# Conversion of the first weights, place of the fp32 pieces, and h before y in a chain of clustered attention and two wide layers

## The chip, the cores and the metric

The kernel runs on one core of a Trainium2 chip. The metric is the device time of one execution in microseconds (us). Before the change the median of three runs is 830.09 us (829.56 to 830.41). The engines are TensorE (PE in the profile; its weight loads are PEld), VectorE (DVE), ScalarE (ACT), GpSimd (POOL), and SyncE (SP), which here only issues DMAs.

## The reference, cut to what matters

```python
# attention: q, k, v of shape (2, 8, 768, 64), 16 centroids for each head
q_assign = argmax(q_n @ c_n.T); k_assign = argmax(k_n @ c_n.T)
scores = where(q_assign == k_assign, q @ k.T / sqrt(64), -1e9)
attn = exp(scores - max) / (sum + 1e-9)
x = (attn @ v) laid out as (1536, 512)
# layer 1: w_in (512, 2048), w_out (2048, 512)
h = x @ w_in;  x = maximum(0.01 * h, h) @ w_out
# layer 2, of the same shapes, with its own weights
h = x @ w_in;  g = P(h) / (Q(h) + 1e-6);  out = g @ w_out
# P = a0 + a1 h + a2 h^2 + a3 h^3,  Q = 1 + |b0||h| + |b1| h^2
```

The weights arrive as 64-bit floats and are converted in the kernel. Each matrix product is made three times, with high and low parts of both operands, to keep fp32 accuracy.

## The kernel before, in words

**Attention.** Two heads make a pair, and there are 8 pairs. A pair has 12 units of 128 query rows, so there are 96 units (`NU`). `run` (line 662) writes the order of work out by hand, one iteration `i` for each unit. In iteration `i` TensorE transposes the normalised probabilities of unit `i - 4` (`trans_p`, tile `pT`, line 519), computes the scores of unit `i + 1` (`scores`, tile `s`, line 477), and does a third of the products with v of a group of three units (`values`, tile `o`, line 552). VectorE takes the maximum of a row (`nm`, line 486) and the low parts of the probabilities (`pl`, line 538). ScalarE does the exponential (`e`, line 497) and the high parts (`ph`, line 532). GpSimd normalises two units at a time (`normalize`, line 511), after one `denom` on ScalarE and one reciprocal on VectorE for both. In two of three iterations the values stand behind the scores; in the third one they stand in front of them.

The preparation of a later pair is cut into pieces. `plan` (line 404) gives each piece an iteration, counted from the pair's first unit, and a slot in it. Slot `"pe"` comes behind the scores and in front of the values; slot `"act"` comes in front of the exponential; slot `"end"` comes last. `trans` (tile `pa`, line 230, three fp32 transposes) and `sims` (line 307, twelve small fp32 products) stand in slot `"pe"`. All `pT`, `pa`, `sims` and `po` tiles take turns in three PSUM buffers (pool `pq`). `trans_out` on ScalarE (line 233) empties a `pa` tile.

**Weights.** The class `Weights` (line 724) holds a queue of conversions. A piece is a DMA of 512 KB into a tile `st`, then four operations (`conv_a` on ScalarE, line 767; `conv_s` and two `conv_c` on VectorE, lines 774 and 780) that leave fp32 in `wf`, and an end: either a split into high and low parts (ScalarE line 787, GpSimd line 790), or a save of the fp32 weights to DRAM. `step()` does one operation of the queue and loads ahead. Before the change the two inward (`wi`) and two outward (`wo`) pieces of the first group are converted and saved during the attention: their loads are issued in iteration 7, one operation follows in two iterations of three, the last one in iteration 59. After the last preparation piece (iteration 84) the `wi` pieces are read back and split. The saved `wo` pieces are read back too, and split at the start of the layers.

**Layers.** Each layer has its inner dimension in groups of four slices of 128 (the first group is halved). A step has one slice and one block of 384 tokens: `make_h` is 12 matmuls into tile `h` (four PSUM buffers), `back` is the product with `w_out` for the step three earlier (`LAG = 3`), 12 matmuls in layer 1 and 9 wider ones in layer 2, into tiles `y0` to `y3` (one buffer each). In between ScalarE and VectorE (and GpSimd in layer 2) make `gh` and `gl` from `h`; these have three buffers each. `collect` on VectorE adds `y` to `acc` after the last slice of a group. The order of each engine is the order of the calls in the loop at line 1100:

```python
            if i >= LAG:
                back(i - LAG)
            if i < NS:
                make_h(i)
            if 0 <= i - 1 < NS:
                start(i - 1)
```

Of the kernel before, what the change touches and what calls it, by code (L numbers as in the profile page):

```python
# [9 lines left out]
F32 = mybir.dt.float32  # L10
F32R = mybir.dt.float32r
I32 = mybir.dt.int32
AF = mybir.ActivationFunctionType
ALU = mybir.AluOpType
# [3 lines left out]
P = 128  # L18
# [11 lines left out]
def clustered_attention_moe_moe2(  # L30
# [14 lines left out]
    nc = tc.nc  # L45
# [11 lines left out]
    BLK = S // 2  # L57
    QT = BLK // P
# [18 lines left out]
    eps = const.tile([P, 1], F32, name="eps")  # L77
# [46 lines left out]
    UP = HP * T  # L124
    NU = NPAIR * UP
# [6 lines left out]
    class Attention:  # L132
# [62 lines left out]
        def prep_pieces(self, p):  # L195
# [192 lines left out]
            def vsplit(h):  # L388
# [14 lines left out]

            plan = [
                (-27, "end", load_qk),
                (-24, "pe", trans, 0, 0),
                (-23, "act", trans_out, 0, 0),
                (-23, "pe", trans, 0, 1),
                (-22, "act", trans_out, 0, 1),
                (-22, "end", split_hi, 0),  # L410
                (-21, "pe", trans, 1, 0),
                (-21, "end", split_lo, 0, 0),
                (-20, "act", trans_out, 1, 0),
                (-20, "pe", trans, 1, 1),
                (-20, "end", split_lo, 0, 1),
                (-19, "act", trans_out, 1, 1),
                (-18, "pe", sims, 0),
                (-19, "end", split_hi, 1),
                (-17, "act", sims_out, 0),
                (-18, "end", split_lo, 1, 0),  # L420
                (-18, "end", place_a, 0),
                (-17, "end", split_lo, 1, 1),
                (-15, "pe", sims, 1),
                (-14, "act", sims_out, 1),
                (-13, "dve", sims_max),
                (-13, "end", place_a, 1),
# [16 lines left out]
            if p == 1:  # L443
                late = {"sims": (-12, -10), "sims_out": (-11, -9), "sims_max": -9, "is_max": -9,
                        "rank": -9, "first": -8, "onehot": (-7, -6)}
# [12 lines left out]
            if p == 2:  # L458
                late = ("trans", "trans_out", "split_hi", "split_lo")
# [38 lines left out]
                un["e"], un["s"][:, 0:S], AF.Exp, bias=un["nm"], accum_out=un["recip"]  # L498
            )

        def denom(self, u):
            un = self.unit[u]
            nc.scalar.activation(un["sum"], un["sum"], AF.Identity, bias=eps)

        def recip(self, u):
            un = self.unit[u]
            nc.vector.reciprocal(un["sum"], un["sum"])  # L507

        def normalize(self, u):
            un = self.unit[u]  # L510
            nc.gpsimd.tensor_scalar(un["e"], un["e"], un["recip"], 1.0, op0=ALU.mult, op1=ALU.mult)  # L511

        def trans_p(self, u, part):
            un = self.unit[u]
            pp = self.pq.tile([P, 512], F32, tag="pT", name="pT")
            n = T // 2
            for kt in range(n):
                k0 = (part * n + kt) * P
                nc.tensor.transpose(pp[:, kt * P:(kt + 1) * P], un["e"][:, k0:k0 + P], ident)  # L519
            un["pT", part] = pp[:, 0:n * P].rearrange("p (t n) -> p t n", t=n)  # L520
# [24 lines left out]
        def values(self, gi, a, z):  # L545
            p, h, half, _ = self.info(gi * QT)
            gr = self.group[gi]
            if a == 0:
                gr["o"] = self.po.tile([P, BLK], F32, tag="o", name="o")
            for n in range(a, z):  # L550
                kt, j = divmod(n, 2)
                nc.tensor.matmul(  # L552
                    gr["o"],
                    lhsT=self.pair[p]["vs"][:, h * T + tile_of(kt), :],
                    rhs=gr["pl" if j else "ph"][:, kt, :],
                    start=n == 0,
                    stop=n == 2 * T - 1,
                )
# [103 lines left out]
        def run(self, extra, fill):  # L662
            TL = 4
            pieces = {}
            for p in range(NPAIR):
                for i, slot, f in self.prep_pieces(p):
                    pieces.setdefault(max(i, -1), {}).setdefault(slot, []).append(f)
            self.startup(*fill)
            first = -1
            last_prep = max(pieces)  # L670
            n_groups = NU // QT
            part = -(-2 * T // QT)
            for i in range(first, NU + TL + 11):
                def go(slot):
                    for f in pieces.get(i, {}).get(slot, []):
                        f()

                gi, r = divmod(i - TL - 3, QT)
                ok = 0 <= gi < n_groups
                live = 0 <= i - TL < NU  # L680
                go("dve0")
                if 0 <= i < NU:
                    self.row_max(i)
                if i % 2 == 0 and 0 <= i - 2 < NU:
                    self.recip(i - 2)
                    self.normalize(i - 2)
                    self.normalize(i - 1)
                if live:
                    self.trans_p(i - TL, 0)
                    self.hi(i - TL, 0)  # L690
                    self.trans_p(i - TL, 1)
                    self.hi(i - TL, 1)
                if ok and r == QT - 1:
                    self.values(gi, part * r, 2 * T)
                    self.merge_copy(gi)
                go("act")
                if 0 <= i < NU:
                    self.exp(i)
                    if i % 2 == 1:
                        self.denom(i)  # L700
                if 0 <= i + 1 < NU:
                    self.scores(i + 1)
                go("pe")
                if ok and r < QT - 1:
                    self.values(gi, part * r, part * (r + 1))
                if live:
                    self.lo(i - TL, 0)
                    self.lo(i - TL, 1)
                if ok and r == QT - 1:
                    self.merge_add(gi)  # L710
                go("dve")
                gd, rd = divmod(i - TL - 3 - 7, QT)
                if rd == 0 and 0 <= gd < n_groups:
                    self.finish(gd)
                go("end")
                if UP // 2 <= i < NU - 2 * UP and i % 3:
                    fill[1].step()
                if i == last_prep:
                    self.pc.close()
                    extra[0]()  # L720
                elif i > last_prep:
                    extra[1]()

    class Weights:
        def __init__(self, pools):
# [148 lines left out]
            else:  # L874
                weights.add((which, n), weight_source(n, which), which, n % 2, WIDE)

    def queue_scratch(n):
        for which in ("wi", "wo"):
            src = weight_source(n, which)
            t = dram.tile([P, src.shape[1], src.shape[2] // WW], F32, name=f"scratch_{which}{n}")  # L880
            weights.add((which, n), src, which, n % 2, WIDE, store=t)
            scratch[n, which] = t
# [3 lines left out]
    with tc.manual_schedule():  # L886
# [13 lines left out]
        def open_start():  # L900
            def slot(tag):
                def stage():
                    t = xp.tile([P, NCT * BLK], F32, tag=tag, name="xst")
                    return t[:, 0:WR * 1024].bitcast(I32), t[:, WR * 1024:WR * 1536]

                weights.wst.append({"stage": stage, "used": 0, "room": 1})

            if WIDE:
                for j in range(NB // 2, NB):
                    slot(f"xh{j}")  # L910
                    slot(f"xl{j}")
                queue_scratch(0)

        def open_weights(which, par, **kw):
            wpools[which, par] = wctx.enter_context(
# [8 lines left out]
            open_stage("wsta", side="right")  # L924
            queue_group(0)

        def early_step():
            weights.step(1)

        weights = Weights(wpools)  # L930
        with ExitStack() as actx:
# [168 lines left out]
        for i in range(NS + LAG):  # L1100
            if i < NS and steps[i][1:] == (0, 0):
                n1 = steps[i][0] + 1
                begin, total = i, 0
                count = NB * groups[n1 - 1][2]
                if n1 < len(groups):
                    queue_group(n1)
                    if WIDE and n1 + NG - 1 > NG0 and n1 + NG - 1 < len(groups):
                        queue_scratch(n1 + NG - 1)
                    total = weights.pending()
            if i >= LAG:  # L1110
                back(i - LAG)
            if i < NS:
                make_h(i)
            if 0 <= i - 1 < NS:
                start(i - 1)
            if 0 <= i - 2 < NS and rational(i - 2):
                hi(i - 2)
                lo(i - 2)
            if later:
                next_x()  # L1120
            if i >= LAG:
                collect(i - LAG)
            if 0 <= i - 1 < NS and rational(i - 1):
                ratio_end(i - 1)
            due = total * min(i - begin + 1, count - 1) // (count - 1)
            weights.step(max(0, due - (total - weights.pending())))
            if i < LAG and weights.waits_for(("wo", 0)):
                weights.step(4)
            if i == LAG - 2:
                while weights.waits_for(("wo", 0)):  # L1130
                    weights.step()
# [29 lines left out]
```

## Time and profile before

| | us |
|---|---|
| median of three runs | 830.09 |
| the profiled execution, whole | 830.46 |
| its span in the profile | 828.7 |
| PE busy | 797.1 (96%) |
| DVE busy | 649.1 (78%) |
| ACT busy | 533.3 (64%) |
| POOL busy | 398.8 (48%) |

The span has four stages: start-up to about 40 us, attention to about 281 us, layer 1 to about 545 us, layer 2 to the end. Busy times are sums of the durations of instructions. Consecutive matmuls overlap, so the start of a matmul after the start of the one before says more of the pace than its duration. A time in square brackets on a timeline row is the idle time of that engine before the instruction and what ended it.

### The profile page before, as it was taken

Reading aid. Unit: us, or ns where it says so; the run is one execution under the profiler, and the core shown is the slowest. Engines: PE = TensorE matmul, PEld = TensorE weight load, DVE = VectorE, ACT = ScalarE, POOL = GpSimd, SP = SyncE. Lnnn points to the kernel's source line nnn. Section 1 sums busy time; section 2 is a strip of 40 time slices with the busy share of each in tenths; the row PEclk is TensorE's granted clock in tenths of the full one; section 3 lists DMA queues with packets and bytes.
Section 4 is the critical chain, followed back from the end, with each engine's and each line's share of the span. In section 5 each row is a group of like instructions: output and inputs, shape, how many; then the busy total and the mean of one; then the engine's idle time right before and its main releaser. Section 6 shows DMA issues by size and latency. Waiting matters only on the chain.

```text
span 828.7 us, 13356 instructions
## 1 busy us (share of the span) xinstructions
PE 797.1 (96%) x4545; PEld 740.7 (89%) x4545; DVE 649.1 (78%) x1232; ACT 533.3 (64%) x1131; POOL 398.8 (48%) x428
## 2 busy tenths in 40 slices
PE   5898999999999899999999999999999999999997
PEld 4887898898888899999999999997889888988995
DVE  6579989989999557766567556758888878888887
ACT  4588988988989544544253345447666667766664
POOL 5557877877665422331031024256555555554442
PEclk9999999999999999999999999999999999999999
DMA  3775745645410223435544454431111110100112
GB/s 102 175 207 116 169 103 117 170 97 124 106 36 26 102 85 120 131 124 169 165 147 155 141 189 130 150 89 27 35 30 28 38 39 26 26 1 1 40 39 76
DMA packets 42835, 79.80 MB, mean 96 GB/s; under 512 B 5392, under 2 KB 25360, under 8 KB 42768
## 3 DMA queue, kind: packets, MB, share of 16 engines
q1 hardware_dynamic: 42768, 78.96, 33.9%
q8 instruction: 36, 0.59, 0.3%
q14 instruction: 31, 0.25, 0.1%
HBM read 50.37 MB, written 10.49 MB: 73 GB/s over the span
## 4 chain that ended last, share of the span: by engine, by line
PE 50%; POOL 15%; DVE 14%; ACT 10%; issue 8%; DMA 2%; SPq 1%; POOLq 0%; DVEq 0%; ACTq 0%
PE y L961 18%; PE h L961 17%; POOL z L1013 6%; PE o L552 5%; PE pT L519 4%; POOL z L1010 4%; PE s L477 3%; DVE pl L538 3%; DVE nm L486 3%; ACT ln L1026 2%; PE sims L307 2%; ACT r L1027 2%; POOL wol L790 2%; POOL wil L790 2%; DMA st<-in_moe_w_in_dram 1%
## 5 line engine op out<-in xcount | busy, mean ns | idle before, releaser
L961 PE MATMUL h<-xh,wil 128*128 128x384 f32 x512 | 172.2, 336 | 0.0
L961 PE MATMUL h<-xh,wih 128*128 128x384 f32 x512 | 171.9, 336 | 0.0
L961 PE MATMUL h<-xl,wih 128*128 128x384 f32 x512 | 171.8, 336 | 0.0
L995 DVE TENSOR_TENSOR gl<-h,gh 128x384 fp32r<-128x384 f32 x128 | 70.8, 553 | 85.6 <-ACT gh L990 68.0
L511 POOL TENSOR_SCALAR e<-e,sum 128x768 f32<-128x768 f32 x96 | 88.6, 936 | 61.5 <-DVE sum L507 44.4
L790 POOL TENSOR_TENSOR wil<-wf,wih 128x512 fp32r<-128x512 f32 x32 | 41.6, 1308 | 143.8 <-ACT wih L787 143.8
L538 DVE TENSOR_TENSOR pl<-pT,ph 128x384 fp32r<-128x384 f32 x192 | 97.2, 545 | 16.6 <-ACT ph L532 15.5
L961 PEld LDWEIGHTS h<-xl,wih 128*128 128x128 f32 x512 | 96.2, 188 | 2.7
L961 PEld LDWEIGHTS h<-xh,wih 128*128 128x128 f32 x512 | 96.2, 188 | 2.5
L486 DVE TENSOR_REDUCE nm<-s 128x1 f32<-128x768 f32 x96 | 90.9, 947 | 7.3 <-PE s L477 6.8
L961 PEld LDWEIGHTS h<-xh,wil 128*128 128x128 f32 x512 | 96.2, 188 | 0.0
L999 ACT ACTIVATE h<-h 128x384 f32<-128x384 f32 x64 | 30.4, 476 | 98.6 <-PE h L961 98.6
L532 ACT CAST ph<-pT 128x384 fp32r<-128x384 f32 x192 | 82.4, 481 | 17.4 <-PE pT L519 16.2
L497 ACT ACTIVATE e<-s,nm 128x768 f32<-128x768 f32 x96 | 87.3, 909 | 9.4 <-DVE nm L486 5.8
L990 ACT CAST gh<-h 128x384 fp32r<-128x384 f32 x128 | 61.6, 482 | 40.4 <-DVE h L1034 38.3
L961 PE MATMUL y<-gh,woh 128*128 128x384 f32 x256 | 86.1, 336 | 0.1
L961 PE MATMUL y<-gl,woh 128*128 128x384 f32 x256 | 85.8, 335 | 0.2 <-DVE gl L995 0.2
L961 PE MATMUL y<-gh,wol 128*128 128x384 f32 x256 | 85.9, 336 | 0.0
L519 PE MATMUL pT<-ident,e 128*128 128x128 f32 x576 | 81.7, 278 | 2.7 <-DVE pl L538 2.7
L1010 POOL TENSOR_SCALAR z<-y,abv 128x384 f32<-128x384 f32 x64 | 43.2, 676 | 77.6 <-ACT y L1006 70.4
L961 PE MATMUL y<-woh,gh 128*128 128x512 f32 x192 | 76.6, 399 | 2.5 <-ACT gh L990 1.5
L961 PE MATMUL y<-woh,gl 128*128 128x512 f32 x192 | 76.6, 399 | 1.3 <-DVE gl L995 1.0
(104 smaller groups left out, 1855.3 us busy)
## 6 DMA issues: line engine op xcount, KB each, us to landing
st<-in_moe_w_in_dram SPq DMA_DIRECT2D x30, 512.0 KB, 4.6
st<-in_moe_w_out_dram SPq DMA_DIRECT2D x30, 512.0 KB, 4.6
a<-hl SPq DMA_DIRECT2D x56, 192.0 KB, 3.7
b<-hl SPq DMA_DIRECT2D x28, 192.0 KB, 6.0
wf<-scratch_wi SPq DMA_DIRECT2D x14, 256.0 KB, 3.1
wf<-scratch_wo SPq DMA_DIRECT2D x14, 256.0 KB, 3.1
qraw<-in_q_dram SPq DMA_DIRECT2D x16, 192.0 KB, 3.1
kraw<-in_k_dram SPq DMA_DIRECT2D x16, 192.0 KB, 3.2
```

The lines of the kernel that those rows point to most:

```text
L486: nc.vector.reduce_max(un["nm"], un["s"][:, 0:S], axis=AX.X, negate=True)
L497: nc.scalar.activation(un["e"], un["s"][:, 0:S], AF.Exp, bias=un["nm"], accum_out=un["recip"])
L511: nc.gpsimd.tensor_scalar(un["e"], un["e"], un["recip"], 1.0, op0=ALU.mult, op1=ALU.mult)
L519: nc.tensor.transpose(pp[:, kt * P:(kt + 1) * P], un["e"][:, k0:k0 + P], ident)
L532: nc.scalar.copy(un["hi", part], un["pT", part])
L538: nc.vector.tensor_tensor(self.group[gi]["pl"][:, part * n:(part + 1) * n, i * P:(i + 1) * P], un["pT", part], f32(un["hi", part]), op=ALU ...
L790: nc.gpsimd.tensor_tensor(hold["l"][:, i:i + wr, :], hold["wf", i], f32(hold["h"][:, i:i + wr, :]), op=ALU.subtract,)
L961: nc.tensor.matmul(o, lhsT=l, rhs=r, start=(first and idx == 0), stop=(last and idx == n - 1),)
L990: nc.scalar.copy(d["gh"], d["h"])
L995: nc.vector.tensor_tensor(d["gl"], d["h"], f32(d["gh"]), op=ALU.subtract)
L1010: nc.gpsimd.tensor_scalar(d["z"], d["y"], abv[:, 1:2], abv[:, 0:1], op0=ALU.mult, op1=ALU.add)
L1013: nc.gpsimd.tensor_tensor(d["z"], d["z"], d["y"], op=ALU.mult)
```

## The change

The change has five parts.

1. `trans` and `sims` move from slot `"pe"` to a new slot `"pa"`, which is called behind the values (and behind the two `lo` of VectorE). `onehot_t` (tile `po`) stays in `"pe"`.
2. During the attention only the two `wi` pieces of the first group are converted and saved. Their loads are issued in iteration 6; one operation follows in every third iteration from 15 on. The two `wo` pieces are loaded from the input after iteration 84 and converted in place: one `conv_a` falls into iteration 86, the other seven operations into iterations 100 to 106.
3. The last two units have a `denom` and a reciprocal of their own; unit 94 is normalised one iteration earlier on GpSimd, unit 95 on VectorE.
4. The transposed probabilities of unit 95 use the buffers of the scores, and the last group's `o` uses a buffer of `pq` instead of the single one.
5. In the layers `make_h(i)` stands in front of `back(i - 3)`.

```diff
             plan = [
                 (-27, "end", load_qk),
-                (-24, "pe", trans, 0, 0),
+                (-24, "pa", trans, 0, 0),
                 (-23, "act", trans_out, 0, 0),
-                (-23, "pe", trans, 0, 1),
+                (-23, "pa", trans, 0, 1),
...
-                (-20, "pe", trans, 1, 1),
+                (-20, "pa", trans, 1, 1),
...
-        def denom(self, u):
+        def denom(self, u, alone=False):
             un = self.unit[u]
-            nc.scalar.activation(un["sum"], un["sum"], AF.Identity, bias=eps)
+            x = un["recip"] if alone else un["sum"]
+            nc.scalar.activation(x, x, AF.Identity, bias=eps)
...
-            pp = self.pq.tile([P, 512], F32, tag="pT", name="pT")
+            pp = self.ring("pT") if u == NU - 1 else self.ptile("pT")
...
             if a == 0:
-                gr["o"] = self.po.tile([P, BLK], F32, tag="o", name="o")
+                if (gi + 1) * QT == NU:
+                    gr["o"] = self.ptile("o")[:, 0:BLK]
+                else:
+                    gr["o"] = self.po.tile([P, BLK], F32, tag="o", name="o")
...
-                if i % 2 == 0 and 0 <= i - 2 < NU:
+                if NU - 1 <= i <= NU:
+                    self.recip(i - 1, True)
+                    self.normalize(i - 1, (nc.gpsimd, nc.vector)[i - NU + 1])
+                elif i % 2 == 0 and 0 <= i - 2 < NU:
...
                     self.exp(i)
-                    if i % 2 == 1:
+                    if i >= NU - 2:
+                        self.denom(i, True)
+                    elif i % 2 == 1:
                         self.denom(i)
...
                 if live:
                     self.lo(i - TL, 0)
                     self.lo(i - TL, 1)
+                go("pa")
                 if ok and r == QT - 1:
                     self.merge_add(gi)
...
-                if UP // 2 <= i < NU - 2 * UP and i % 3:
+                if i == UP // 2:
+                    fill[1].preload(4)
+                if UP + 3 <= i < NU - 2 * UP and i % 3 == 0:
                     fill[1].step()
...
-                    extra[1]()
+                    extra[1](i >= NU + TL)
...
-                queue_scratch(0)
+                queue_scratch(0, ("wi",))
...
-        def early_step():
-            weights.step(1)
+        def early_step(late):
+            if late or weights.waits_for(("wi", 0)):
+                weights.step(1)
...
+            if i < NS:
+                make_h(i)
             if i >= LAG:
                 back(i - LAG)
-            if i < NS:
-                make_h(i)
```

## Rows read from the trace of the kernel before

**Rows 1.** Busy time by stretch: start:end, length, then PE, PEld, DVE, ACT, POOL, PEclk.
```profile
40.00:236.00 196.00, 187.62 (x1278) 170.39 (x1279) 180.86 (x332) 170.35 (x413) 140.86 (x160) 0.99 0.55 130
236.00:281.00 45.00, 41.22 (x264) 36.78 (x264) 37.11 (x70) 37.65 (x89) 28.99 (x34) 1.00 0.10 29
281.00:545.00 264.00, 263.63 (x1514) 262.97 (x1513) 168.74 (x324) 120.47 (x237) 62.03 (x50) 1.00 0.45 145
545.00:600.00 55.00, 53.10 (x268) 47.22 (x267) 44.95 (x78) 35.67 (x69) 35.40 (x37) 1.00 0.13 38
800.00:828.70 28.70, 23.43 (x111) 19.43 (x109) 21.33 (x39) 13.95 (x26) 8.40 (x10) 1.00 0.15 55
```

**Rows 2.** TensorE's waits, 40 to 236 us: total us, times, longest.
```profile
PE pa L230 <- ACT x L233: 3.5, 11, 0.5
```

**Rows 3.** Timeline of TensorE at one such wait: start, duration, what.
```profile
103.08 0.55 PE L230 MATMUL pa<-ident,kraw 128*128 128x128 f32 x3 [0.51 <-ACT x L233]
103.39 0.42 PE L552 MATMUL o<-ph,vs 128*128 128x384 f32 x1
103.64 0.34 PE L552 MATMUL o<-pl,vs 128*128 128x384 f32 x1
103.82 0.35 PE L552 MATMUL o<-ph,vs 128*128 128x384 f32 x1
```

**Rows 4.** VectorE's longest waits, 40 to 236 us.
```profile
DVE pl L538 <- ACT ph L532: 12.0, 21, 1.8
```

**Rows 5.** Timeline of TensorE: the same piece in four successive pairs.
```profile
80.52 0.47 PE L365 MATMUL po<-identr,oh 128*96 128x128 f32 x4
...
111.28 0.47 PE L365 MATMUL po<-identr,oh 128*96 128x128 f32 x4
...
142.99 0.48 PE L365 MATMUL po<-identr,oh 128*96 128x128 f32 x4
...
174.21 0.47 PE L365 MATMUL po<-identr,oh 128*96 128x128 f32 x4
```

**Rows 6.** Timeline of ScalarE: the first conversion of a weight piece.
```profile
49.20 0.67 ACT L767 ACTIVATE xst<-xst 128x512 f32<-128x512 f32 x1 [1.10 <-DMA xst<-in_moe_w_in_dram]
```

**Rows 7.** Timeline of VectorE and GpSimd: conversions of the outward pieces.
```profile
127.39 0.41 DVE L774 TENSOR_SCALAR xst<-xst 128x512 int32<-128x512 int32 x1
...
128.91 1.81 POOL L511 TENSOR_SCALAR e<-e,sum 128x768 f32<-128x768 f32 x2 [0.24 <-DVE sum L507]
...
130.04 0.95 DVE L774 TENSOR_SCALAR xst<-xst 128x512 int32<-128x512 int32 x1
...
135.77 0.68 DVE L780 SCALAR_TENSOR_TENSOR xst<-xst 128x512 int32<-128x512 int32 x1
```

**Rows 8.** Timeline at the end of attention.
```profile
251.25 3.33 SPq L761 DMA_DIRECT2D wf<-scratch_wo  x2
...
254.34 0.62 PE L477 MATMUL s<-a 128*128 128x512 f32 x2 [0.66 <-ACT e L497]
...
273.77 0.44 PE L552 MATMUL o<-ph,vs 128*128 128x384 f32 x1 [0.40 <-DVE xf L573]
...
278.64 0.45 PE L552 MATMUL o<-ph,vs 128*128 128x384 f32 x1 [1.16 <-DVE xf L573]
```

**Rows 9.** DMA issues, page part 6: count, size, us to landing.
```profile
st<-in_moe_w_in_dram SPq DMA_DIRECT2D x30, 512.0 KB, 4.6
```

**Rows 10.** Timeline in layer 2: its first y, a collect near the end, the last y.
```profile
556.28 0.47 PE L961 MATMUL y<-woh,gh 128*128 128x512 f32 x1 [0.81 <-ACT r L1027]
...
810.89 1.88 DVE L1079 TENSOR_TENSOR acc<-y,acc 128x512 f32<-128x512 f32 x3
...
822.47 0.50 PE L961 MATMUL y<-woh,gh 128*128 128x512 f32 x1 [1.21 <-ACT gh L990]
```

**Rows 11.** Busy time and granted clock in two short stretches; columns as in rows 1.
```profile
44.00:48.00 4.00, 4.00 (x22) 3.79 (x22) 2.20 (x4) 2.26 (x6) 2.25 (x3) 0.57 0.99 253
60.00:62.00 2.00, 2.00 (x15) 1.68 (x14) 2.00 (x6) 1.81 (x5) 1.33 (x2) 1.00 1.10 191
```

More of the change, by code (lines that the diff above doesn't have):

```diff
@@ L405, in prep_pieces @@
                 (-27, "end", load_qk),
-                (-24, "pe", trans, 0, 0),
+                (-24, "pa", trans, 0, 0),
                 (-23, "act", trans_out, 0, 0),
-                (-23, "pe", trans, 0, 1),
+                (-23, "pa", trans, 0, 1),
                 (-22, "act", trans_out, 0, 1),
                 (-22, "end", split_hi, 0),
-                (-21, "pe", trans, 1, 0),
+                (-21, "pa", trans, 1, 0),
                 (-21, "end", split_lo, 0, 0),
                 (-20, "act", trans_out, 1, 0),
-                (-20, "pe", trans, 1, 1),
+                (-20, "pa", trans, 1, 1),
                 (-20, "end", split_lo, 0, 1),
                 (-19, "act", trans_out, 1, 1),
-                (-18, "pe", sims, 0),
+                (-18, "pa", sims, 0),
                 (-19, "end", split_hi, 1),
@@ L422, in prep_pieces @@
                 (-17, "end", split_lo, 1, 1),
-                (-15, "pe", sims, 1),
+                (-15, "pa", sims, 1),
                 (-14, "act", sims_out, 1),
@@ L499, in exp, with recip, normalize @@
             )
-        def denom(self, u):
+        def denom(self, u, alone=False):
             un = self.unit[u]
-            nc.scalar.activation(un["sum"], un["sum"], AF.Identity, bias=eps)
-        def recip(self, u):
+            x = un["recip"] if alone else un["sum"]
+            nc.scalar.activation(x, x, AF.Identity, bias=eps)
+        def recip(self, u, alone=False):
             un = self.unit[u]
-            nc.vector.reciprocal(un["sum"], un["sum"])
-        def normalize(self, u):
+            x = un["recip"] if alone else un["sum"]
+            nc.vector.reciprocal(x, x)
+        def normalize(self, u, eng=nc.gpsimd):
             un = self.unit[u]
-            nc.gpsimd.tensor_scalar(un["e"], un["e"], un["recip"], 1.0, op0=ALU.mult, op1=ALU.mult)
+            eng.tensor_scalar(un["e"], un["e"], un["recip"], 1.0, op0=ALU.mult, op1=ALU.mult)
         def trans_p(self, u, part):
             un = self.unit[u]
-            pp = self.pq.tile([P, 512], F32, tag="pT", name="pT")
+            pp = self.ring("pT") if u == NU - 1 else self.ptile("pT")
             n = T // 2
@@ L875, in queue_group, with queue_scratch @@
                 weights.add((which, n), weight_source(n, which), which, n % 2, WIDE)
-    def queue_scratch(n):
-        for which in ("wi", "wo"):
+    def queue_scratch(n, whiches=("wi", "wo")):
+        for which in whiches:
             src = weight_source(n, which)
```

## The prediction

> **What bounds the kernel now.** I read the busy time by stretch first, then TensorE's waits in the stretches where it is not full, then timelines around these waits. The reader is to see in [rows 1] that TensorE is nearly always busy: in layer 1 it is idle for 264.00 - 263.63 = 0.4 us, at the start of layer 2 for 55.00 - 53.10 = 1.9 us, in the last 28.7 us for 5.3 us. The work of TensorE stays the same, so the change can only win idle time. Most of that lies in attention: 196.00 - 187.62 = 8.4 us up to 236 us, and 45.00 - 41.22 = 3.8 us from there to the layers. But VectorE is busy there for 180.86 of 196 us, 92%, and ScalarE for 87%. Wherever TensorE stops waiting, VectorE is the next limit; its own waits of 12.0 us [rows 4] are the room that it has. The start-up before 40 us is left as it was.
>
> **Part 1, the fp32 pieces behind the values.** TensorE waits 11 times, 3.5 us in all, in front of a `pa` tile for ScalarE to empty the previous one [rows 2]. Each pair has two such places: `trans(0,1)` and `trans(1,1)` ask for their buffer in the same iteration in which `trans_out` empties one. Both lie in iterations with values behind the scores, where four products with v start 0.17 to 0.18 us apart [rows 3]: 0.7 us of work that now covers a wait of at most 0.5 us. The pairs 3 to 7 gain, two places each; the eleventh wait belongs to pair 2, before there are any values. So ten waits of 0.32 us go, 3.2 us. Second, the product behind a `pa` piece starts its successor 0.25 us later instead of 0.18 us [rows 3]; in the new place more fp32 transposes follow, which already pay this step in front of the scores. That is 10 x 0.08 = 0.8 us. `sims` stand in iterations whose values come first, so nothing moves for them, and `trans_out` comes an iteration later as before, so the pieces behind it are not late. What is late next is VectorE: of its 12.0 us of waiting part 1 asks for 4.0. Bounds: nothing, if VectorE takes it all back, and 10 x (0.5 + 0.08) = 5.8 us, if every wait is as long as the longest. A loss I exclude: the transposes only pass work that was ready. I take -4.0 us.
>
> **Part 2, the conversions.** Between the same piece of successive pairs [rows 5] lie 30.76, 31.71 and 31.22 us. In the first interval no weight is converted; in the second fall the two `conv_a`, both `conv_s` and the first `conv_c` of the two outward pieces, in the third their last `conv_c` and the saves. Against the first interval they cost 0.95 + 0.46 = 1.4 us, which go. The inward pieces keep their cost in other iterations. Their first `conv_a` stops ScalarE for 1.10 us until its load lands [rows 6], because load and conversion stand in the same iteration; now nine iterations lie between them. TensorE feels less than that; I take 0.4 us. Together -1.8 us. Bounds: nothing, if TensorE is the limit anyway, and what leaves the engines, VectorE's 2 x (0.41 + 2 x 0.68) [rows 7] = 3.5 us and the 1.1 us of ScalarE, 4.6 us.
>
> At the end of attention it costs something. ScalarE holds TensorE back there (0.66 us for an exponential in [rows 8]), and in iteration 86 it gets a `conv_a` of 0.67 us [rows 6] more; queued behind it are the high parts that the values wait for. I take +0.6 us, between 0 and 1.0 us with the extra `denom`. The load of that piece needs 4.6 us [rows 9] and is issued about two iterations ahead; it is hidden if SP's queue isn't held (a rival below). The other seven operations come after iteration 100, beside the last values, when VectorE and ScalarE run dry. VectorE's 3.5 us of them can begin when the last products are merged, about when the first h starts, and the first y comes four h later in the new order, 4 x 264 / 128 = 8.2 us, so the split of the first outward piece has some 4 us left. I take nothing.
>
> **Parts 3 and 4, the last units.** The last group's products wait 1.16 us for the merge that frees the only `o` buffer [rows 8]; with a buffer of its own that goes. But the normalisation of unit 95 now stands on VectorE in front of the low parts of unit 92 and the merge for which the products at 273.77 already wait 0.40 us [rows 8]. It takes 768 / 512 x 0.41 = 0.6 us by the TENSOR_SCALAR of 512 columns; the same instruction beside GpSimd's normalisation took 0.95 us [rows 7], which would make 1.4 us. GpSimd is then at work on the merged x, so I take 1.0 us. Net -0.2 us, bounds -1.2 and +0.3 us.
>
> [...]
>
> **Part 5, h before y.** A unit gets one more y between its h and its own y. The wait for the first y of layer 1 and its neighbours go (0.2 of the 0.4 us idle), and most of the 1.9 us at the start of layer 2 [rows 1, 10], where the chain from h to `gl` grows: 1.5 us. At the end I give 0.2 us only, although the last y waits 1.21 us [rows 10]: the last collect before it takes VectorE 1.88 us, and in both orders the same work of TensorE lies between the y that it waits for and the y of a later unit. Nothing inside the layers is left to win. It could cost where y has one buffer: a collect must be through within one h, as before. Together -1.9 us, bounds -3.5 us (with the whole 1.21 and 0.4) and 0.
>
> **The sum.** -4.0 - 1.8 + 0.6 - 0.2 - 1.9 = -7.3 us. The profiled execution took 830.46 us, 1.8 us more than its span, and 0.4 us more than the median of the runs: 823.2 us against its own time, 822.8 us against the median, which I predict.
>
> **Rivals.** (a) VectorE is the limit of attention, and part 1 gives nothing: -3.3 us, 826.8 us. For it speak the 92%; against it, that part of VectorE's 12.0 us of waiting follows just the iterations in which TensorE is late. (b) The wait moves to the load: today's loads of the outward pieces were issued at 251.25 us [rows 8], when their buffers came free. If the new one is issued only then, ScalarE, which comes to its `conv_a` in that same iteration, stands for the 4.6 us of the load [rows 9]: 827.4 us. Against it: the new load goes into `st`, which nobody has used. (c) All gains are at their bounds, because VectorE's waits were all caused by TensorE: -5.8 - 4.6 + 0 - 1.2 - 3.5 = -15.1 us; half way from the forecast is 819 us. [...]
>
> **How the numbers follow.** Forecast 48% (820.8 to 825.2 us by itself), (a) 20%, (b) 10%, (c) 12%, (d) 4%, something I don't see 6%, half of it no change and half slower. What a measurement can tell from no change is 0.2%, 1.7 us. Faster: forecast, (a), (b) and (c), less 3% for (a) or (b) with smaller gains elsewhere: 87%; the same 6%; slower 7%. The range leaves out the far half of (c), (d) and the unseen: 818.8 to 828.0 us.
>
> **What would show it.** After the change TensorE's waits for `x` behind `pa` should be gone but one; the intervals of [rows 5] should be near 30 us, all three; VectorE's waits for `ph` should be some 4 us shorter. If `pT` or `s` waits grow by as much, (a) holds. [...] The last products of attention should start without a wait, and those before them later against their scores. Layer 2 should begin without waits of TensorE, and its last y still wait about 1 us. I am wrong if attention is not shorter by 3 us or more.

## The result

The changed kernel takes 819.21 us, the median of four runs (819.02 to 821.04). The kernel before, run beside it, took 829.56 to 830.41 us in three runs and 1565.84 us in a fourth, which is left out: the ratio is 0.9877 [0.9862, 0.9892]. The forecast was 822.8 us, in a range of 818.8 to 828.0. The profiled execution took 819.38 us with a span of 817.6 us, 11.1 us less than the one before; the forecast for it was 7.3 us less. The direction was right and the time lies in the range, but three of the terms were off: part 5 and part 2 gave more than forecast, parts 3 and 4 lost where they should have won.

Busy time of the changed kernel by stretch, with the columns of [rows 1]; the stretches end at the same places of the program, give or take 1 us:

```profile
40.00:230.00 190.00, 186.60 (x1297) 171.66 (x1296) 175.33 (x329) 171.53 (x418) 142.38 (x162) 1.00 0.54 126
230.00:275.00 45.00, 41.27 (x252) 36.62 (x251) 37.47 (x70) 37.47 (x88) 25.57 (x31) 0.96 0.13 41
275.00:539.00 264.00, 264.00 (x1519) 264.00 (x1518) 177.32 (x329) 119.68 (x239) 63.78 (x52) 1.00 0.44 145
539.00:594.00 55.00, 55.00 (x285) 50.82 (x284) 45.91 (x80) 37.11 (x72) 35.27 (x37) 1.00 0.13 45
789.00:817.60 28.60, 23.74 (x111) 19.44 (x109) 21.96 (x40) 13.44 (x26) 8.41 (x10) 1.00 0.15 56
```

TensorE's idle time in attention fell from 8.4 us to 3.4 us, that at the start of layer 2 from 1.9 us to nothing, and the end of attention (the second row) is no better: 3.7 us idle against 3.8 us, and now with a granted clock of 0.96.

TensorE's waits from 40 to 230 us, for [rows 2], in the same columns:

```profile
PE s L477 <- ACT e L497: 0.9, 3, 0.5
PE pT L521 <- DVE pl L540: 0.6, 1, 0.6
PE pa L230 <- ACT x L233: 0.3, 1, 0.3
```

Of the eleven waits for `x` one is left, as forecast. VectorE's waits for [rows 4] did not get shorter:

```profile
DVE pl L540 <- ACT ph L534: 13.1, 29, 0.9
```

The pieces of [rows 5], in TensorE's timeline of the changed kernel:

```profile
76.73 0.48 PE L365 MATMUL po<-identr,oh 128*96 128x128 f32 x4 [0.15 <-ACT sv L318]
...
107.43 0.48 PE L365 MATMUL po<-identr,oh 128*96 128x128 f32 x4
...
137.92 0.48 PE L365 MATMUL po<-identr,oh 128*96 128x128 f32 x4
...
167.58 0.48 PE L365 MATMUL po<-identr,oh 128*96 128x128 f32 x4
```

The intervals are 30.70, 30.49 and 29.66 us instead of 30.76, 31.71 and 31.22 us. There are seven such pieces behind the start-up, and with them, the start of the first h and that of the last y block the whole gain can be placed (starts in the two traces; the forecast is that of the parts which fall into the stretch; "seventh piece to the first h" is the end of attention). The 0.7 us of the first row are not the change's: in a kernel whose attention is that of before (experiment 2) the first piece starts at 46.45 us.

| stretch of TensorE | before, us | after, us | difference | forecast |
|---|---|---|---|---|
| start to the first piece | 47.22 | 46.56 | -0.7 | none |
| first to seventh piece | 186.35 | 179.24 | -7.1 | -5.8 (parts 1, 2) |
| seventh piece to the first h | 47.27 | 49.17 | +1.9 | +0.6 (`conv_a`), -0.2 (parts 3, 4) |
| first h to the last y block | 541.63 | 536.32 | -5.3 | -1.9 (part 5) |

### The profile page after: what moved, and what is told of

It reads as the page before. It is cut to its first block, busy times and chain, and to the rows that moved or that the text cites. A ratio compares the mean times of both kernels' runs of the same rounds, so it can differ in the third digit from the quotient of the medians.

```text
span 817.6 us, 13355 instructions
## 1 busy us (share of the span) xinstructions
PE 793.9 (97%) x4545; PEld 743.0 (91%) x4545; DVE 652.6 (80%) x1234; ACT 530.2 (65%) x1132; POOL 397.2 (49%) x427
## 4 chain that ended last, share of the span: by engine, by line
PE 61%; POOL 13%; DVE 9%; ACT 8%; issue 7%; DMA 0%; POOLq 0%; SPq 0%; DVEq 0%; ACTq 0%
PE h L975 20%; PE y L975 20%; PE s L477 6%; PE o L557 6%; POOL z L1027 5%; PE pT L521 5%; POOL z L1024 4%; DVE pl L540 3%; PE sims L307 2%; POOL wol L803 2%; ACT ln L1040 2%; ACT r L1041 2%; DVE nm L486 2%; POOL wil L803 2%; ACT ph L534 1%
## 5 line engine op out<-in xcount | busy, mean ns | idle before, releaser
L513 POOL TENSOR_SCALAR e<-e,sum 128x768 f32<-128x768 f32 x95 | 86.7, 924 | 53.4 <-DVE sum L509 36.5
L793 DVE SCALAR_TENSOR_TENSOR wf<-st,wf 128x512 int32<-128x512 int32 x124 | 83.3, 723 | 0.0
L803 POOL TENSOR_TENSOR wol<-wf,woh 128x512 fp32r<-128x512 f32 x32 | 41.9, 1322 | 72.7 <-ACT woh L800 55.6
```

The costliest lines, as they stand in the source:

```text
L513: eng.tensor_scalar(un["e"], un["e"], un["recip"], 1.0, op0=ALU.mult, op1=ALU.mult)
L793: nc.vector.scalar_tensor_tensor(wi, hold["st", i][:, :, :, 1 - w], sc, wi, op0=op, op1=ALU.bitwise_or)
L803: nc.gpsimd.tensor_tensor(hold["l"][:, i:i + wr, :], hold["wf", i], f32(hold["h"][:, i:i + wr, :]), op=ALU.subtract,)
```

## The experiments

Eleven runs, ten of other kernels and one of the changed kernel again, each timed beside the kernel before; the ratios are to that one on the same chip. Edits are to the changed kernel unless said otherwise.

**1. Part 5 undone (y_first).**

```diff
-            if i < NS:
-                make_h(i)
             if i >= LAG:
                 back(i - LAG)
+            if i < NS:
+                make_h(i)
```

> The changed kernel with y in front of h again (part 5 undone). Theory: a stop of TensorE costs what lies between the starts of its matmuls, about twice the idle time that the profile gives, and the layers lose all that they won between the first h and the last y: 819.2 + 5.3 = 824.5 us, 3.4 us of it in the first steps of layer 2. Rival, the forecast's own term from idle times: 819.2 + 1.9 = 821.1 us.

Measured: 825.5 us (823.35 to 825.99), ratio 0.9932 [0.9908, 0.9956]; from the first h to the last y block 542.55 us, 6.2 us more than with the part. TensorE's waits at the start of layer 2 are back, and the one in front of the last y:

```profile
551.15 0.47 PE L975 MATMUL y<-woh,gh 128*128 128x512 f32 x1 [0.82 <-ACT r L1041]
...
556.44 0.51 PE L975 MATMUL y<-woh,gl 128*128 128x512 f32 x1 [0.33 <-DVE gl L1009]
...
560.71 0.50 PE L975 MATMUL y<-woh,gh 128*128 128x512 f32 x1 [0.27 <-ACT gh L1004]
...
561.78 0.50 PE L975 MATMUL y<-woh,gl 128*128 128x512 f32 x1 [0.33 <-DVE gl L1009]
...
817.57 0.50 PE L975 MATMUL y<-woh,gh 128*128 128x512 f32 x1 [1.21 <-ACT gh L1004]
```

**2. Part 5 alone (only_h_first):** the kernel before, with `make_h` in front of `back` as its only edit.

> The kernel before with one edit, h in front of y (part 5 alone). Theory from start to start: attention as before, first h to last y 541.6 - 5.3 = 536.3 us, the time 830.1 - 5.3 = 824.8 us. By the forecast's idle times: 828.2 us. Rival: part of the 5.3 us needs the other parts (the conversion of the first group stands elsewhere): between the two.

Measured: 825.95 us, ratio 0.9961 [0.9944, 0.9977]. Its runs spread from 824.27 to 829.87 us, so the place is read from the profile (824.53 us): first h to last y block 536.25 us, 5.4 us less than before, and no wait of TensorE between 550 and 562 us; the six intervals of attention make 186.58 us, as before. Part 5 is worth 5.3 to 6.2 us, some three times its term, with or without the other parts. The 0.9 us more of experiment 1 come mostly from the first y of layer 1, which waits there for `gh` for 0.96 us and in the kernel before for less than 0.1 us: with part 2 the outward conversions stand in front of that `gh` on VectorE and ScalarE, and it is the order of part 5 that hides them.

**3. Part 1 undone (pieces_in_front).**

```diff
                 go("pe")
+                go("pa")
 ...
-                go("pa")
                 if ok and r == QT - 1:
```

> The changed kernel with trans and sims in front of the values again (part 1 undone, all else kept). Theory: each of the ten places costs its gap from start to start, 0.5 us and more, and 0.08 us: 819.2 + 6 = 825.2 us, and the waits of TensorE for x come back with 3 us or more. The forecast's term from idle times: 819.2 + 4.0 = 823.2 us. Rival: VectorE is the limit of attention, so that the order of the pieces gives nothing: 819.2 us.

Measured: 822.44 us (819.29 to 823.25), ratio 0.9889 [0.9854, 0.9923]. First to seventh piece 182.87 us, 3.6 us more; how much of that is the clock was not shown: the mean granted clock of this profile is 0.99, that of the changed kernel's 0.998. The medians differ by 3.2 us, and one of the four runs (819.29 us) is as fast as the changed kernel. Most of the waits come back:

```profile
PE pa L230 <- ACT x L233: 2.6, 8, 0.5
```

I had come to think that part 1 carried nearly all of attention's gain, some 6 us; that fell. Its term of 4.0 us in the prediction was right in sum. By intervals the part gives 1.1, 0.0, 0.3, 1.1 and 1.0 us. The second and third interval, where it gives little, are those in which VectorE has the inward pieces' conversions. One such place in the changed kernel, a conversion and then the transposes that wait behind VectorE's late low parts:

```profile
97.88 0.69 DVE L793 SCALAR_TENSOR_TENSOR xst<-xst 128x512 int32<-128x512 int32 x1
...
100.23 0.92 PE L521 MATMUL pT<-ident,e 128*128 128x128 f32 x6 [0.64 <-DVE pl L540]
```

**4. Part 2 undone (conversions_as_before).**

```diff
-                if i == UP // 2:
-                    fill[1].preload(4)
-                if UP + 3 <= i < NU - 2 * UP and i % 3 == 0:
+                if UP // 2 <= i < NU - 2 * UP and i % 3:
                     fill[1].step()
 ...
-                queue_scratch(0, ("wi",))
+                queue_scratch(0)
 ...
-            if late or weights.waits_for(("wi", 0)):
-                weights.step(1)
+            weights.step(1)
```

> The changed kernel with the weights of the first group converted as before the change (inward and outward pieces during attention, loads and first operation in the same iteration; part 2 undone, all else kept). If part 1 gave 4.0 us up to the last onehot piece, the conversions gave 7.8 - 4.0 = 3.8 us there, less 0.5 us that the end of attention pays for the conv_a in iteration 86: 819.2 + 3.3 = 822.5 us. If part 1 gave 6 us: 819.2 + 1.3 = 820.5 us, close to the forecast's net 1.2 us. Rival: the conversions lie beside other work: 819.2 us or under it.

Measured: 822.6 us (822.03 to 823.66), ratio 0.9899 [0.987, 0.9929]. First to seventh piece 184.33 us, 5.1 us more than in the changed kernel; behind the seventh piece it wins 1.9 us back, mostly by a granted clock that stays at 1.00 there (experiment 7). The parts are not additive: part 1 alone is worth 186.35 - 184.33 = 2.0 us, part 2 alone 186.35 - 182.87 = 3.5 us, both 7.1 us. Seven profiles with the attention of the changed kernel up to there agree on 179.2 to 179.6 us, so the difference is clear. Against the kernel before, part 1 alone wins nothing in the first and third interval (34.17 us for 33.30, 31.72 for 31.71), where the conversions are dense, and 0.9 to 1.1 us in each of the second, fourth and fifth. TensorE's waits of that stretch are now for VectorE:

```profile
PE pT L521 <- DVE pl L540: 4.1, 6, 1.3
```

**5. All four conversions, but the loads early (both_spread):** as experiment 4, with `preload(4)` kept and the operations in two of three iterations from `UP + 3` on.

> The changed kernel with both the inward and the outward pieces of the first group converted during attention, as much work as before the change, but with the loads issued in iteration 6 and the operations begun in iteration 15 (two of three iterations). The run with the old conversions took 5.1 us more between iterations 7 and 79 and 1.9 us less from there to the first h. Theory 1, the time of the operations counts (from iteration 7 on they stand in the first iterations beside the work of pair 2): most of the first interval comes back, 34.2 to about 31 us, and the time is 822.6 - 3 = 819.6 us. Theory 2, the amount counts (VectorE's 3.5 us and ScalarE's 1.3 us of the outward pieces): only the 0.4 us of the load go, 822.2 us.

Measured: 824.62 us (823.66 to 828.87), ratio 0.9946 [0.993, 0.9963]. The theory that the time at which the operations run decides fell; how many of them stand in one interval decides. Busy time of two successive intervals, with and without conversions on VectorE (columns of [rows 1]):

```profile
79.87:113.63 33.76, 30.39 (x209) 27.37 (x209) 32.42 (x59) 27.39 (x67) 25.47 (x28) 1.00 0.46 112
113.63:143.30 29.67, 29.53 (x209) 27.56 (x209) 27.21 (x52) 27.62 (x68) 23.64 (x28) 1.00 0.61 144
```

and VectorE's timeline in the first of them:

```profile
88.34 1.38 DVE L793 SCALAR_TENSOR_TENSOR xst<-xst 128x512 int32<-128x512 int32 x1
...
91.89 1.42 DVE L793 SCALAR_TENSOR_TENSOR xst<-xst 128x512 int32<-128x512 int32 x1
```

With 52 instructions VectorE is free for 2.5 us of 29.67; with 59, two of them at 1.38 and 1.42 us twice the 0.68 us of [rows 7], it is busy for 96% and sets the pace. The other dense interval, 143.30 to 177.08 us, takes 33.78 us, with VectorE busy for 31.84 us of it, 94%. The kernel had a second fault of its own: its four loads stood in front of another transfer on SP's queue, and TensorE waited 3.96 us for `b` at 57.27 us, with a granted clock of 0.60 from 54 to 62 us. So its total says less than the intervals.

**6. The inward operations one iteration later (inward_other_phase):** `i % 3 == 1` for `i % 3 == 0`.

> The changed kernel with the conversions of the inward pieces in iterations 16, 19, 22, ... instead of 15, 18, 21, ...: the same amount, the same distance, one iteration later. Theory, the place of an operation counts: a conv_c with two operands in SBUF takes 0.7 us by itself and 1.2 to 1.4 us beside GpSimd, and where a pa tile holds the third buffer of the transposes TensorE waits for VectorE behind it. In the run with both pieces spread each interval with conv_c in such iterations was 3 us longer. Here the inward pieces' four conv_c fall into one such interval: up to 3 us longer between iterations 19 and 43, the time 819.2 + 2 to 3 = 821 to 822 us, and TensorE waits for pl with 2 us or more. Rival, only the amount counts: 819.2 us, intervals within 0.3 us of the changed kernel's.

Measured: 817.65 us (815.05 to 818.36), ratio 0.9854 [0.9834, 0.9875]. I asked whether it matters beside which of the other operations a conversion stands. No effect shows: 29.85, 30.39 and 30.77 us for the first three intervals, against 30.17, 30.70 and 30.49 us. The test is weak, because the four `conv_c` took only 0.68 to 0.97 us in their new places. The gain in the total, 1.8 us against the changed kernel on the same chip, comes mostly from the end of attention in the two profiles (47.71 us from the seventh piece to the first h, against 49.04 us; experiment 7).

**7. Unit 95's normalisation on GpSimd (unit95_gpsimd).**

```diff
-                    self.normalize(i - 1, (nc.gpsimd, nc.vector)[i - NU + 1])
+                    self.normalize(i - 1, nc.gpsimd)
```

> The changed kernel with one edit: unit 95 is normalised on GpSimd, as unit 94, instead of on VectorE. Theory: on VectorE it took 1.36 us beside a subtraction of GpSimd and held back the low parts whose buffer the next transposes wait for (a wait of TensorE of 1.48 us), and that pause is what brought the granted clock down to 0.77 to 0.80 from 266 to 274 us. Then both go: the wait falls to 0.3 us, the clock stays at 1.00, and the time is 819.2 - 2.5 = 816.7 us. Rival: the slow clock comes from the other edits of the end (buffers of unit 95 and of the last o), and only some 1.0 us of the wait goes: 818.2 us, the clock still low.

Measured: 817.32 us (816.65 to 818.44), ratio 0.9836 [0.9806, 0.9865]; seventh piece to first h 46.67 us instead of 49.17 us. The changed kernel's timeline at that place:

```profile
264.73 1.00 POOL L593 TENSOR_TENSOR xl<-xf,xh 128x384 fp32r<-128x384 f32 x1
264.78 1.36 DVE L513 TENSOR_SCALAR e<-e,sum 128x768 f32<-128x768 f32 x1
...
266.07 1.01 DVE L540 TENSOR_TENSOR pl<-pT,ph 128x384 fp32r<-128x384 f32 x2
...
266.67 0.55 PE L521 MATMUL pT<-ident,e 128*128 128x128 f32 x3 [1.48 <-DVE pl L540]
...
267.59 0.45 PE L557 MATMUL o<-ph,vs 128*128 128x384 f32 x1 [0.38 <-DVE xf L578]
```

VectorE normalises for 1.36 us beside GpSimd's subtraction; the two low parts queued behind it come late, and TensorE stands for 1.48 us. Then its granted clock falls (columns of [rows 1]):

```profile
267.60:273.60 6.00, 6.00 (x29) 5.67 (x30) 3.17 (x7) 2.61 (x7) 0.00 (x0) 0.72 0.00 0
```

With the normalisation on GpSimd, where it takes 0.90 us, the same place reads:

```profile
264.45 1.02 DVE L540 TENSOR_TENSOR pl<-pT,ph 128x384 fp32r<-128x384 f32 x2 [0.20 <-ACT ph L534]
...
265.06 0.55 PE L521 MATMUL pT<-ident,e 128*128 128x128 f32 x3 [0.39 <-DVE pl L540]
...
265.21 0.90 POOL L513 TENSOR_SCALAR e<-e,sum 128x768 f32<-128x768 f32 x1
```

```profile
266.00:271.00 5.00, 5.00 (x32) 4.65 (x33) 3.63 (x8) 3.06 (x7) 0.20 (x2) 1.00 0.00 2
```

The pause does not always bring the lower clock. In the profile of experiment 6 TensorE stands for the same 1.48 us at the same place and goes on at 1.00:

```profile
265.90 0.55 PE L521 MATMUL pT<-ident,e 128*128 128x128 f32 x3 [1.48 <-DVE pl L540]
```

```profile
266.80:271.80 5.00, 4.97 (x31) 4.63 (x32) 3.62 (x8) 3.03 (x7) 0.05 (x1) 1.00 0.00 0
```

There the stretch to the first h is 47.71 us long. So the pause costs 47.71 - 46.67 = 1.0 us, and the clock 49.17 - 47.71 = 1.5 us where it falls. Seven profiles have this pause at this place: the clock fell behind it in five, to 0.72 over 6 us in each (the changed kernel, its second run, experiments 1, 3 and 5), and stayed at 1.00 in two (experiments 4 and 6). Of the six without it, the kernel before, experiment 7 and best read 1.00 there; in experiments 2, 8 and 9 the products with v there start mostly 0.17 to 0.18 us apart, as in the kernel before; at a clock of 0.50 those of the changed kernel start 0.32 us apart.

**8. Part 3 undone, part 4 kept (old_tail_new_buffers):** the last two units are normalised as a pair on GpSimd again, with the added buffers.

> The changed kernel with units 94 and 95 normalised as before (one denom and one reciprocal for both, both on GpSimd; part 3 undone), the buffers of part 4 kept. Theory: all that part 3 brings is the pause of TensorE, and part 4 by itself gives the forecast's 1.2 us: the same as with unit 95 on GpSimd, 816.6 to 817.3 us, the clock at 1.00, no wait of over 0.5 us for pl in the last units. Rival: the earlier normalisation of unit 94 is worth something by itself: 0.9 us (one normalisation) more, 818 us.

Measured: 817.6 us (816.32 to 818.52), ratio 0.9852 [0.9835, 0.9868]; seventh piece to first h 46.47 us. Against experiment 7 (46.67 us) part 3 is worth nothing even without its VectorE piece, and with it, it loses 1.2 us (where the clock stays, as in experiment 6) to 2.7 us. Part 4 is what wins: 47.27 us before, 46.47 us here, although the `conv_a` of iteration 86 is still inside (experiment 9); without that, 46.02 us (best), which makes 1.25 us for the wait of 1.16 us of [rows 8].

**9. No `conv_a` in iteration 86 (unit95_no_early_conv):** experiment 7 and

```diff
             if late or weights.waits_for(("wi", 0)):
+                if not late:
+                    weights.turn = 0
                 weights.step(1)
```

> The kernel with unit 95 on GpSimd, and with the first operation on an outward piece kept out of iteration 86, so that both inward pieces are split in iterations 85 and 86 as before the change. Theory: the conv_a of 0.7 us there held ScalarE, and TensorE behind it, for 0.45 us: 46.67 us from the last onehot piece to the first h become 46.2 us, the time 816.2 us. Rival: ScalarE has room there and it is nothing, 816.7 us; or the operations that are left after iteration 100 then hold the first y, 817 us or more.

Measured: 816.04 us (813.98 to 818.28), ratio 0.9835 [0.9815, 0.9855]; seventh piece to first h 46.12 us. By the profiles the early conversion costs 46.67 - 46.12 = 0.55 us, as the term of 0.6 us said; the runs' times spread too far to show it. Its load was in time: in the changed kernel SP issues it 7.7 us ahead, and ScalarE does not wait for it.

```profile
235.87 0.90 SPq L768 DMA_DIRECT2D st<-in_moe_w_out_dram  x2
...
243.57 0.69 ACT L780 ACTIVATE wf<-st 128x512 f32<-128x512 f32 x1
```

**10 and 11. Both improvements together (best), beside the changed kernel run again (changed_again).** best leaves out part 3 (as experiment 8) and the early `conv_a` (as experiment 9).

> The changed kernel once more, beside the two others on the same chip: 819.2 us. What is asked is the pause of 1.5 us in the last units: if the granted clock falls behind it in this profile too, 49.2 us from the last onehot piece to the first h; if not, 47.7 us and a time of some 817.7 us.

> The changed kernel with part 3 undone (units 94 and 95 normalised together on GpSimd), the buffers of part 4 kept, and no operation on an outward piece in iteration 86. Theory: both gains at the end of attention add: 46.5 - 0.5 = 46.0 us from the last onehot piece to the first h, 3.2 us less than the changed kernel, 816.0 us. Rival: they share one place (ScalarE's queue in the last iterations), 816.5 us or more.

Measured on the same chip: changed_again 819.47 us (818.89 to 821.44), 0.9886 [0.9871, 0.99]; best 816.55 us (815.96 to 817.19), 0.9846 [0.9832, 0.9861]. The ranges do not meet: 2.9 us of the changed kernel's time are a loss that it need not have. The profile of best has 46.02 us from the seventh piece to the first h, and a clock of 1.00 there; in changed_again it fell to 0.72 once more. Between best and experiment 9 these runs show no difference.

## Why the prediction came out as it did

The sum landed near for partly the wrong reasons, and in that there is luck: part 5 gave 3.4 us more than its term, parts 1 and 2 together 1.3 us more and the start-up 0.7 us, while parts 3 and 4 took 1.65 us back.

**Part 5 (-1.9 us; it was -5.3 us): mechanism right, size wrong.** This is the term that failed most. I took the idle time of [rows 1] as what a stop costs. The kernel before shows what it misses, at the start of layer 2:

```profile
560.84 0.40 PE L961 MATMUL y<-wol,gh 128*128 128x512 f32 x1
561.57 0.50 PE L961 MATMUL y<-woh,gl 128*128 128x512 f32 x1 [0.33 <-DVE gl L995]
561.90 0.40 PE L961 MATMUL y<-woh,gh 128*128 128x512 f32 x1
```

Without a stop such products start 0.23 us apart, each while the previous one is still counted as busy. Here the distance is 0.73 us, and the next one is 0.33 us: 0.60 us are lost where the view counts 0.33 us. Taken from start to start, against 2.085 us for an undisturbed block of h or of y, the kernel before loses 1.35 us in layer 1, 3.56 us at the start of layer 2, 3.10 us in the rest of it and 1.94 us in the tail; the changed one loses 0.36, 0.13, 2.48 and 1.68 us. So layer 1 gave 1.0 us instead of 0.2 (0.6 us of it at its first y), the start of layer 2 3.4 us instead of 1.5, and "nothing inside the layers is left to win" was wrong by 0.6 us. Experiments 1 and 2 put all of it on this part. The tail was judged rightly, 0.3 us for 0.2. Its last waits got shorter, but the profile's chain that ends last runs in both kernels from a collect of VectorE (800.09 us after the change, 810.89 us before) through VectorE, ScalarE and GpSimd to the last `gh`, and takes 11.2 us to the last y after the change and 11.6 us before:

```profile
808.75 0.50 PE L975 MATMUL y<-woh,gl 128*128 128x512 f32 x1 [0.33 <-DVE gl L1009]
...
811.29 0.50 PE L975 MATMUL y<-woh,gh 128*128 128x512 f32 x1 [0.65 <-ACT gh L1004]
```

**Part 1 (-4.0 us): right in sum, not in its spread.** Undone it costs 3.6 us (experiment 3), with both of its mechanisms in the traces: ten of the eleven waits are gone, and no product with v stands behind a `pa` piece any more. But its gain comes where VectorE has no conversions; where it has, VectorE takes it back, as rival (a) said. How the gain divides into the 3.2 us and the 0.8 us no run separates. The sign that I named with it was wrong, however: VectorE's waits for `ph` should have lost 4 us, and rose from 12.0 us in 21 to 13.1 us in 29. VectorE's work fell as much as the time did: it is busy for 180.86 of 196 us before and for 175.33 of 190 us after, 92% both times.

**Part 2 (-1.8 us; with part 1 it was -7.1 us for -5.8 us): too small, and not additive.** I priced the outward conversions in intervals two and three of [rows 5] against the first one shown there, in which no weight is converted. The largest gain lay ahead of these rows, between the first and the second piece, where the inward pieces were converted densely in the kernel before: 33.30 us there, 30.17 us after, when VectorE's part of that work had moved into the next two intervals. "The inward pieces keep their cost in other iterations" is the sentence that failed; the 0.4 us for the first load was not measured by itself. One interval of each kernel, first before, then after:

```profile
47.22:80.52 33.30, 30.76 (x209) 27.43 (x208) 30.18 (x56) 28.09 (x68) 21.02 (x23) 1.00 0.66 165
```

```profile
46.56:76.73 30.17, 29.83 (x209) 27.62 (x209) 27.44 (x52) 28.08 (x69) 21.50 (x25) 1.00 0.64 154
```

An operation of the conversion was not paid by its length here but by whether VectorE's room held it. The kernel before shows one that it did not hold: 1.21 us on VectorE, beside GpSimd's work, and then TensorE's wait for the low part behind it.

```profile
67.30 1.21 DVE L780 SCALAR_TENSOR_TENSOR xst<-xst 128x512 int32<-128x512 int32 x1
...
69.99 0.92 PE L519 MATMUL pT<-ident,e 128*128 128x128 f32 x6 [1.19 <-DVE pl L538]
```

What the six operations of two pieces on VectorE cost depended on their density here. At one operation in three iterations they cost the changed kernel 1.9 us over two intervals (30.70 and 30.49 us, against 29.66 us for one without), at two of three 4.1 us in one (experiment 5). With the fp32 pieces in front (experiment 3) the spread ones cost nothing: 30.72 and 30.81 us, against 30.80 us. That the order in time decides was tried and fell (5); for the neighbour no effect showed (6). This is also why the parts are not additive: where VectorE converts densely it takes back what part 1 wins, so each alone gives less than its share of the sum. Rival (a) was half right: VectorE is the limit, but only in the intervals with conversions.

**The end of attention (+0.6 us for `conv_a`): right;** 0.55 us by experiment 9, 0.45 us between experiment 8 and best. For the other seven operations I took nothing, and that holds only together with part 5 (experiment 1). Rival (b), the late load, did not come.

**Parts 3 and 4 (-0.2 us; it was +1.45 us): wrong sign.** Part 4 did what it should; the last group no longer waits for the merge. The step that failed is the price of the normalisation on VectorE: 1.0 us was taken and 1.36 us measured, close to the bound of 1.4 us, and I counted it once, where two low parts and the merge were queued behind it and TensorE stood for 1.48 us. It ran beside a subtraction of 1.00 us on GpSimd; 0.6 us, from the 0.41 us of 512 columns [rows 7], was the estimate for the operation alone, and no run has it alone, so what GpSimd's work added is not shown by itself. The rest is the clock, which no term held at this place: 1.5 us.

**(d), 4% for a kernel slower by TensorE's clock at the moved transposes, did not come.** The loss it stood for was the author's estimate, and no run shows it: from 40 to 230 us the granted clock is 1.00, with nine fp32 transposes in a row at twenty places from 59 us on, ten of which the kernel before had already. What a longer row would do is not shown, since nine in a row take only 0.9 us here (91.95 to 92.84 us), among other matmuls. Where the clock did fall, at the end of attention, TensorE had stood still for 1.48 us before.

**Rival (c), all gains at their bounds (819 us half way), is where the time landed, for another reason:** part 5 went beyond its bound of 3.5 us, while parts 3 and 4 went beyond theirs the other way.

What stays open: why the same pause of 1.48 us at the end of attention is followed by a lower clock in five of seven profiles and by 1.00 in two. The length of the pause alone does not say: another one of 1.48 us, at 94.86 us of experiment 5, left the clock at 1.00. Near 43 us pauses of 0.96 us (the kernel before) and 0.98 us (experiment 8) were followed by a slow stretch: a clock of 0.57 from 44 to 48 us in the kernel before [rows 11], and six transposes that take 1.52 us there in both, against 0.81 and 0.82 us near 48.3 us, while behind a longer pause of 1.16 us (experiment 6) the six take 0.85 us. Open too is what of part 3's purpose a kernel without the VectorE piece could use, since experiments 7 and 8 differ by less than they can tell.

## What to carry to other kernels

Price a stop of a pipelined engine from start to start against an undisturbed stretch, and not by its recorded idle time: here 1.9 us of idle were 3.6 us. Extra work on an engine with little room was paid here by its density per stretch (1.9 us over two intervals, 4.1 us in one), so read the busy share of the densest stretch, not the mean, and look for it ahead of the rows that happen to repeat well. An instruction that is moved onto another engine is priced with all that is queued behind it there: here 1.36 us on VectorE made TensorE stand for 1.48 us.

## What the runs showed of the hardware

- Some VectorE operations took about twice as long beside GpSimd's work: SCALAR_TENSOR_TENSOR of 512 columns 0.68 us alone (kernel before, 76.59 and 139.06 us), 1.21, 1.38 and 1.42 us beside it (kernel before, 67.30 us; experiment 5, 88.34 and 91.89 us); TENSOR_SCALAR of 768 columns 1.36 us (changed kernel), where 0.6 us is the estimate for it alone, from 0.41 us for 512 columns [rows 7]. GpSimd's subtraction beside it kept its 1.00 us. At another place it was the other way round: the same SCALAR_TENSOR_TENSOR kept 0.68 us, and GpSimd's normalisation beside it took 1.52 us instead of 0.91 us (kernel before, 73.15 us).
- A pause of TensorE of 1.48 us in the last units was followed by a lower granted clock in five of seven profiles, 0.72 over 6 us in the changed kernel and 0.50 from 268.6 to 271.6 us of it: 1.5 us more. Pauses of 0.3 to 0.4 us at the same place were followed by 1.00 (the kernel before, experiment 7, best), and so was one of 1.16 us near it in the kernel before.
